# First expert product of an attention and mixture-of-experts kernel: eight quarter products against Strassen's seven

## The chip, the cores and the metric

The kernel runs on one core of a Trainium2 chip. The metric is the device time of one execution in microseconds (us); the time before is the median of three runs. A core has TensorE (PE, matrix products), VectorE (DVE), ScalarE (ACT), GpSimd (POOL) and SyncE (SP, which here only issues DMAs). Each works through its own queue in order and waits on semaphores for the others.

## The reference

A windowed attention (plain windows for half of the heads, dilated ones for the others) feeds a mixture of eight experts, of which each token takes its two best:

```python
    noisy_logits = logits + noise_scale * noise
    top2 = np.argpartition(-noisy_logits, 2, axis=1)[:, :2]
    ...
    for e in range(E):
        for k in range(2):
            mask = top2[:, k] == e
            ...
            h = np.maximum(x[mask] @ w1[e], 0.0)
            out[mask] += top2_w[mask, k, None] * (h @ w2[e])
```

There are 4608 tokens of 512 features; W1 is 512 x 1024 and W2 1024 x 512 per expert. All is float32. The two expert products are made in float32r on TensorE from a high and a low part of each operand: high x high + high x low + low x high, so three matmuls stand for one.

## The kernel before, in words

**Stages.** Attention comes first (slots 0 to 51 of an order written by hand, about 235 us in the profile), with gating and the writing of the token table `tab` threaded through it. Then come eight experts, one after the other, each with a fixed capacity of tokens (`CAPS`: 1216 three times, 1184 twice, 1152 three times), cut into tiles of 128 tokens and into three blocks of 3, 4 and 2 to 3 tiles (`BLS`).

**An expert's work.** For each tile `gather` (L751) fetches rows of x with indirect DMAs from GpSimd: four of 32 rows each for experts 1 to 7 (L766), two for expert 0 (L758), after a small `pace` instruction (L297) that waits for a recent result. `xsplit` (L771) transposes the tile (DVE, L783; TensorE for expert 0, L780), casts it to the high part (ACT, L785) and subtracts for the low part (DVE, L786). `up` (L802) makes the first product of a block: for each of eight slices of 128 hidden features twelve matmuls into one PSUM bank (L814), then a ReLU on ACT (L818) and the low part on DVE (L820). `down` (L868) calls `down_tile` (L841) per tile: 24 matmuls of 512 columns (L856), the scaling into y on DVE (L865), and puts a scatter into `pend`, which adds the rows to `out` by an indirect DMA from GpSimd (L833) and is emitted one tile later. A last tile of at most 64 rows is "stacked": 16 matmuls instead of 24. Weights come through two staging buffers `ws` (L683, L698) and are split into high (ACT, L694, L707) and low (DVE, L696, L709).

**What sets the order.** Each engine executes in the order in which the Python program emits. That order is a planner's: `plan(t, f)` (L884) puts f on a heap, `tick(cols)` (L891) advances a clock `now` by cols/2400 us whenever matmuls are emitted, and emits what has come due. For experts 1 to 7 `plan_x` (L794) plans one gather per 9 us and the split of a tile `LAG` = 15 us later; blocks 0 of x have a buffer of their own, blocks 1 and 2 another each, so a block is split while others are multiplied. The experts are interleaved: up block 0, down block 2 of the expert before, up 1, down 0, up 2, down 1. y has a pool of three buffers (L1048). The index loads of the next expert (L735 to L740) and their copies on GpSimd (L745) are planned in the same way.

**Expert 0.** Its tokens are gathered as the gating goes on: tiles 0 to 2 from the first units of attention, tiles 3 to 6 (up to `SPLITS[2]`) after the third unit, the rest at the end of gating. Its first block needs tiles 0 to 2.

Of the kernel before, what the change touches and what calls it, by code (L numbers as in the profile page):

```python
# [9 lines left out]
F32 = mybir.dt.float32  # L10
F32R = mybir.dt.float32r
# [24 lines left out]
NWARM = 24  # L36
SL_W1 = 5
# [3 lines left out]
US_W2 = 3.0, 3.5  # L41
LAG = 15
US_X = (17, 52)
# [3 lines left out]
def attention_moe_kernel(ctx, tc, qt, kp, kd, vpl, vdl, w_gate, w_noise, noise, w1, w2, out, CAPS=(1216, 1216, 1216, 1184, 1184, 1152, 1152, 1152), SPLITS=(0, 384, 896)):  # L47
# [13 lines left out]
    NBL = [max(bl[i][3] for bl in BLS) for i in range(3)]  # L61
# [192 lines left out]
    def setup_c():  # L254
# [3 lines left out]
        free = [late["stage"].tile([128, FF], I32, name="free", tag="ws") for _ in range(2)]  # L258
# [421 lines left out]
    ST = {}  # L680
    W1, W2 = {}, {}

    def stage_w1(e, kc):  # L683

        s = late["stage"].tile([128, FF], F32, name="ws", tag="ws")
        sync.dma_start(s, w1[0][128 * kc:128 * kc + 128] if type(e) is int else
                       row(w1, e).rearrange("(q c d) f -> c q d f", q=4, c=4)[kc])
# [10 lines left out]
    def stage_w2(e, fc):  # L698
        s = late["stage"].tile([128, 2, DM], F32, name="ws2", tag="ws")
        sync.dma_start(s, row(w2, e)[256 * fc:256 * fc + 256].rearrange("(c p) d -> p c d", p=128))  # L700
        ST[2, fc] = s

    def split_w2(fc):
        s = ST.pop((2, fc))
        a = late["wp2"].tile([128, 2, DM], F32R, name=f"w2h{fc}")
        b = late["wp2"].tile([128, 2, DM], F32R, name=f"w2l{fc}")
        scalar.copy(a, s)  # L707
        W2[fc] = (a, b)
# [513 lines left out]
```

## Time and profile before

| | |
|---|---|
| median of three runs | 1046.4 us (1044.11 to 1051.29) |
| span of the profiled execution | 1109.4 us |
| span of attention, expert 0, experts 1 to 7 | 235.7, 129.5, 734.2 us |
| mean granted TensorE clock | 0.966 |
| HBM read, written | 92.11 MB, 39.54 MB |

The profile is of one execution, whose own time is its span of 1109.4 us, 63 us over the median of the runs; the page gives no other time for it. The views used below: the page (busy time of each engine), the busy time by stretches (for each stretch its length, then busy time and number of instructions of PE, PEld, DVE, ACT and POOL, the granted clock, the DMA share and GB/s; for one source line PE and PEld alone), the groups by form (count, busy us, mean ns, idle time before them and what ended it), and the timeline (start, duration, what, and in brackets the idle time before it with its releaser).

### The profile page before, as it was taken

Reading aid. Unit: us, or ns where it says so; the run is one execution under the profiler, and the core shown is the slowest. Engines: PE = TensorE matmul, PEld = TensorE weight load, DVE = VectorE, ACT = ScalarE, POOL = GpSimd, SP = SyncE. Lnnn points to the kernel's source line nnn. Section 1 sums busy time; section 2 is a strip of 40 time slices with the busy share of each in tenths; the row PEclk is TensorE's granted clock in tenths of the full one; section 3 lists DMA queues with packets and bytes.
Section 4 is the critical chain, followed back from the end, with each engine's and each line's share of the span. In section 5 each row is a group of like instructions: output and inputs, shape, how many; then the busy total and the mean of one; then the engine's idle time right before and its main releaser. Section 6 shows DMA issues by size and latency. Waiting matters only on the chain. (4 is left out here: it accounts for less than half of the span.)

```text
span 1109.4 us, 18401 instructions
## 1 busy us (share of the span) xinstructions
PE 1015.0 (91%) x7278; PEld 853.6 (77%) x7279; DVE 463.9 (42%) x1060; ACT 319.8 (29%) x612; POOL 527.7 (48%) x723
## 2 busy tenths in 40 slices
PE   5896776686999899999999999999999999999996
PEld 3774655465779789878988898788978898888885
DVE  6773535644224444334433433434343344333221
ACT  6673433531113232222222222212231213222110
POOL 6004243356866545664635564455456455553112
PEclk9998887887999999999999999999999999999999
DMA  7798687465243432633353334333433443353123
GB/s 275 254 345 292 193 270 251 122 205 161 44 90 76 102 101 48 139 60 103 65 117 68 97 72 101 82 79 85 97 83 81 104 68 102 62 129 58 32 30 46
DMA packets 77530, 132.91 MB, mean 120 GB/s; under 512 B 29968, under 2 KB 39616, under 8 KB 76160
## 3 DMA queue, kind: packets, MB, share of 16 engines
q1 hardware_dynamic: 55088, 92.55, 26.3%
q0 software_dynamic: 22352, 39.15, 19.6%
q8 instruction: 58, 0.95, 0.4%
q14 instruction: 32, 0.26, 0.1%
HBM read 92.11 MB, written 39.54 MB: 119 GB/s over the span
## 5 line engine op out<-in xcount | busy, mean ns | idle before, releaser
L814 PE MATMUL up<-x,w1h 128*128 128x512 f32 (+4 forms) x1536 | 397.5, 345 | 8.8 <-DVE hl L820 5.8
L766 POOL DMA_INDIRECT g<-xs,ixi x258 | 264.5, 1025 | 84.5 <-issue 79.1
L814 PEld LDWEIGHTS up<-x,w1h 128*128 128x128 f32 x1536 | 272.7, 189 | 36.4 <-DVE hl L820 7.6
L814 PE MATMUL up<-x,w1l 128*128 128x384 f32 (+4 forms) x768 | 264.1, 344 | 1.8 <-DVE w1l L696 1.1
L856 PE MATMUL dn<-w2h,hh 128*128 128x512 f32 x576 | 226.7, 394 | 2.0 <-DVE y L865 1.3
L856 PE MATMUL dn<-w2h,hl 128*128 128x512 f32 x576 | 225.3, 391 | 1.1 <-issue 1.1
L856 PE MATMUL dn<-w2l,hh 128*128 128x512 f32 x576 | 225.5, 391 | 0.6 <-issue 0.6
L820 DVE SCALAR_TENSOR_TENSOR hl<-up,hh 128x384 fp32r<-128x384 f32 (+2 forms) x192 | 106.1, 556 | 228.0 <-ACT hh L818 177.1
L833 POOL DMA_INDIRECT out_rows<-y,ixs x67 | 107.8, 1609 | 189.3 <-DVE y L865 158.3
L818 ACT ACTIVATE hh<-up 128x384 fp32r<-128x384 f32 (+4 forms) x192 | 94.2, 498 | 274.7 <-PE up L814 193.9
L814 PEld LDWEIGHTS up<-x,w1l 128*128 128x128 f32 x768 | 145.7, 190 | 14.7 <-DVE w1l L696 1.8
L856 PEld LDWEIGHTS dn<-w2h,hh 128*128 128x128 f32 x576 | 109.0, 189 | 25.6 <-DVE y L865 2.4
L856 PEld LDWEIGHTS dn<-w2h,hl 128*128 128x128 f32 x576 | 108.8, 189 | 24.0 <-issue 1.1
L856 PEld LDWEIGHTS dn<-w2l,hh 128*128 128x128 f32 x576 | 109.0, 189 | 22.6 <-issue 0.8
L865 DVE TENSOR_SCALAR y<-dn,ixs 128x512 f32<-128x512 f32 x63 | 46.9, 748 | 143.4 <-PE dn L856 114.9
L785 ACT CAST x<-xr 128x512 fp32r<-128x512 f32 x67 | 40.5, 605 | 189.9 <-DVE xr L783 158.5
L619 POOL DMA_INDIRECT tab<-en,si x72 | 72.2, 1002 | 30.7 <-issue 16.4
L696 DVE TENSOR_TENSOR w1l<-ws,w1h 128x1024 fp32r<-128x1024 f32 x32 | 38.8, 1217 | 94.8 <-ACT w1h L694 61.6
L297 POOL COPY spacer<-hh 1x1 f32<-1x1 f32 x72 | 24.2, 336 | 102.0 <-ACT hh L818 101.7
L694 ACT CAST w1h<-ws 128x1024 fp32r<-128x1024 f32 x32 | 33.0, 1048 | 115.9 <-DMA ws<-in_moe_w 115.8
L786 DVE TENSOR_TENSOR x<-xr,x 128x512 fp32r<-128x512 f32 x67 | 44.7, 666 | 18.0 <-ACT x L785 15.9
L783 DVE STREAM_TRANSPOSE xr<-g 128x512 f32<-128x512 f32 x67 | 45.7, 682 | 0.0
(184 smaller groups left out, 856.0 us busy)
## 6 DMA issues: line engine op xcount, KB each, us to landing
ws<-in_moe_w SPq DMA_DIRECT2D x64, 512.0 KB
out_rows<-zero SPq DMA_DIRECT2D x38, 256.0 KB
vd<-in_vdl SPq DMA_DIRECT2D x24, 390.0 KB
vp<-in_vpl SPq DMA_DIRECT2D x16, 585.0 KB
qt<-in_qt SPq DMA_DIRECT2D x14, 576.0 KB
xs<-x SPq DMA_DIRECT2D x24, 256.0 KB
kt<-in_kd SPq DMA_DIRECT2D x16, 320.0 KB
g<-xs,ixi POOLq DMA_INDIRECT x258
```

Source lines behind the costliest of these rows:

```text
L619: ins = gpsimd.indirect_dma_start(out=tab, out_offset=bass.IndirectOffsetOnAxis(ap=si[:, kq, t:t + 1], axis=0), in_=en[:, kq, t], in_offse ...
L696: return lambda: vector.tensor_tensor(b, s, a.bitcast(F32), op=OP.subtract)
L766: gpsimd.indirect_dma_start(out=g[:, j], out_offset=None, in_=xq, in_offset=bass.IndirectOffsetOnAxis(ap=IX[e][1][:, r0 // 32 + j:r0 // 32 ...
L783: vector.transpose(xr[:, :, 0:rn].rearrange("p c (g t) -> p g c t", t=32), g[:, 0:n].rearrange("p g (c d) -> p g c d", d=32))
L785: scalar.copy(xh[:, :, o:o + rn], xr[:, :, 0:rn])
L786: return lambda: vector.tensor_tensor(xl[:, :, o:o + rn], xr[:, :, 0:rn], xh[:, :, o:o + rn].bitcast(F32), op=OP.subtract)
L814: tensor.matmul(p[:, 0:n], lhsT=a[:, 128 * f:128 * f + 128], rhs=b[:, kc, 0:n], start=(i == 0), stop=(i == 11))
L818: scalar.activation(hh[:, f, 0:n], p[:, 0:n], AF.Relu)
L820: vector.scalar_tensor_tensor(hl[:, f, 0:m], p[:, 0:m], 0.0, hh[:, f, 0:m].bitcast(F32), op0=OP.max, op1=OP.subtract)
L833: ins = gpsimd.indirect_dma_start(out=out, out_offset=bass.IndirectOffsetOnAxis(ap=sc[0:rn, t, 1:2], axis=0), in_=y[0:rn], in_offset=None, ...
L856: tensor.matmul(p[0:rn], lhsT=a[:, f, o:o + rn], rhs=b[:, f % 2], start=(i == 0), stop=(i == 23))
L865: vector.tensor_scalar(y[0:rn], p[0:rn], wsc, None, op0=OP.mult)
```

## The change

The product X W1 of a block is made by Strassen's scheme (in the form with fifteen additions) on 2 x 2 quarters: the 512 input features in two halves, the 1024 hidden features in two halves, and each tile's tokens in two halves. Seven quarter products take the place of eight. There are two blocks per expert, of five tiles (`NA`) and of the rest, and expert after expert without interleaving. Sums of quarters are made of W1 (on GpSimd for experts 1 to 7) and of x (on DVE) before the splits; `up` handles the hidden features in four steps j, each with seven products of six matmuls over half of the block's tokens, keeps three partial results per step in SBUF (pool `yt`, four buffers, shared with y), and interleaves the products of two steps. The first tile of `down` is begun inside the end of `up`. x has one buffer for all blocks. W1 is loaded by quarters of its columns. The scaling into y moves from DVE to ACT. Gathers, splits, weights and indices become generators that wait for conditions (a buffer free, an `up` over) and for planner times.

```diff
+US_LOAD = 4.5
+US_GATHER = 4.8
+US_LAG = 9.0
...
-US_W2 = 3.0, 3.5
-LAG = 15
-US_X = (17, 52)
+NA = 5
...
-        cuts = [0, 3, 7, len(tl_)]
-        BLS.append([(cuts[i], cuts[i + 1], 128 * cuts[i], min(cap, 128 * cuts[i + 1]) - 128 * cuts[i]) for i in range(3)])
+        BLS.append([(0, NA, 0, 128 * NA), (NA, len(tl_), 128 * NA, cap - 128 * NA)])
...
+    def stage_w1(e, w, j, kk):
+        s = ST[w, j, kk] = stage()
+        d = s[:, 0:512].rearrange("p (i h f) -> p i h f", i=2, h=2)
...
+        for q in range(4):
+            src = row(w1, e)[128 * q:128 * q + 128].rearrange("(h k d) (i j f) -> d i h k j f", h=2, k=2, i=2, j=4)
+            for i in range(2):
+                sync.dma_start(d[32 * q:32 * q + 32, i], src[:, i, :, kk, j])
+    def sums_w1(w, j, kk, eng):
+        s = ST[w, j, kk]
+        a = s[:, 0:512].rearrange("p (i h f) -> p i h f", i=2, h=2)
+        b = s[:, 512:896].rearrange("p (o f) -> p o f", o=3)
+        eng.tensor_tensor(b[:, 0], a[:, 1, 0], a[:, 1, 1], op=OP.add)
+        eng.tensor_tensor(b[:, 1], b[:, 0], a[:, 0, 0], op=OP.subtract)
+        eng.tensor_tensor(b[:, 2], a[:, 0, 1], b[:, 1], op=OP.subtract)
+        eng.tensor_tensor(a[:, 1, 0], a[:, 0, 0], a[:, 1, 0], op=OP.subtract)
+    def split_w1(w, j, kk):
...
+        t = W1[w, j]
+        scalar.copy(t[:, 0, :, kk], s)
+        def low():
+            vector.tensor_tensor(t[:, 1, :, kk], s, t[:, 0, :, kk].bitcast(F32), op=OP.subtract)
+            ready1[w, j] += 1
+        return low
...
-        scalar.copy(xh[:, :, o:o + rn], xr[:, :, 0:rn])
-        return lambda: vector.tensor_tensor(xl[:, :, o:o + rn], xr[:, :, 0:rn], xh[:, :, o:o + rn].bitcast(F32),
-                                            op=OP.subtract)
+        q = ra.rearrange("p c (h t) -> p c h t", h=2)
+        b = r[:, 512:512 + 6 * m].rearrange("p (o k t) -> p o k t", o=3, k=2)
+        vector.tensor_tensor(b[:, 0], q[:, 0:2, 1], q[:, 0:2, 0], op=OP.subtract)
+        vector.tensor_tensor(b[:, 1], q[:, 2:4, 1], b[:, 0], op=OP.subtract)
+        vector.tensor_tensor(b[:, 2], q[:, 2:4, 0], b[:, 1], op=OP.subtract)
+        vector.tensor_tensor(q[:, 0:2, 1], q[:, 2:4, 1], q[:, 0:2, 1], op=OP.subtract)
+        b = b.rearrange("p o k t -> p (o k) t")
+        xa = [x[:, z, 0:8, o:o + m].rearrange("p (h c) t -> p c h t", h=2) for z in range(2)]
+        xb = [x[:, z, 8:14, o:o + m] for z in range(2)]
+        scalar.copy(xa[0], q)
+        scalar.copy(xb[0], b)
+        def low():
+            vector.tensor_tensor(xa[1], q, xa[0].bitcast(F32), op=OP.subtract)
+            vector.tensor_tensor(xb[1], b, xb[0].bitcast(F32), op=OP.subtract)
+            done[e, bi] = done.get((e, bi), 0) + 1
+        return low
...
-        pool = late["xp0" if bi == 0 else "xp"]
-        t = pool.tile([128, 2, 4, NBL[bi]], F32R, name="x", tag="raw" if bi == 0 else f"x{bi}")
-        X[e, bi] = (t[:, 0], t[:, 1])
...
+        X[e, bi] = late["xp"].tile([128, 2, 14, HN], F32R, name="x", tag="x")
...
-            p = late["mps"].tile([128, 512], F32, name="up", tag="up", bufs=3)
-            i = 0
-            for kc in range(4):
-                wh, wl = W1[kc]
-                for a, b in ((wh, xh), (wh, xl), (wl, xh)):
-                    tensor.matmul(p[:, 0:n], lhsT=a[:, 128 * f:128 * f + 128], rhs=b[:, kc, 0:n],
-                                  start=(i == 0), stop=(i == 11))
-                    i += 1
-            tick(12 * n)
-            scalar.activation(hh[:, f, 0:n], p[:, 0:n], AF.Relu)
...
+    def up(e, bi, n, tail=None):
...
+        def mm(p, j, a, b, start):
+            w = W1[e, j]
+            for kk in range(2):
+                for i, (y, z) in enumerate(((0, 0), (0, 1), (1, 0))):
+                    tensor.matmul(p, lhsT=w[:, y, a, kk], rhs=x[:, z, 2 * b + kk, 0:N], start=start and kk == 0 and i == 0,
+                                  stop=kk == 1 and i == 2, skip_group_check=True)
+            tick(6 * N)
+        def keep(p):
+            t = late["yt"].tile([128, 512], F32, name="yt", tag="yt")[:, 0:N]
+            scalar.copy(t, p)
+            return t
...
+        for j in range(5):
+            i = j - 1
+            if j < 4:
+                while e != "o" and ready1.get((e, j), 0) < 2:
+                    tick(600)
+                P[j] = gps.tile([128, 512], F32, name="upg", tag="tin")[:, 0:N] if more and j % 2 else bank("p", 2)
+                mm(P[j], j, 0, 0, True)
+            if i >= 0:
+                high(i, 1, U2[i])
+            if j < 4:
+                S1[j] = keep(P[j])
+            else:
+                part()
+            if i >= 0:
+                mm(P[i], i, 2, 2, False)
+                low(i, 1, U2.pop(i))
+                add(M5[i], P[i])
+            if j < 4:
+                Q[j] = bank("q", 1)
+                mm(Q[j], j, 4, 4, True)
+            else:
+                part()
+            if i >= 0:
+                high(i + 4, 1, M5[i])
+            if j < 4:
+                M5[j] = keep(Q[j])
+                R[j] = bank("r", 1)
+                mm(R[j], j, 1, 1, True)
+            if i >= 0:
+                low(i + 4, 1, M5.pop(i))
+            if j < 4:
+                add(S1[j], R.pop(j))
+            if i >= 0:
+                mm(P[i], i, 3, 6, False)
+                if bi == 1:
+                    free1[i] = e
+            if j < 4:
+                high(j, 0, S1[j])
+            if i >= 0:
+                high(i + 4, 0, P[i])
+            if j < 4:
+                mm(P[j], j, 5, 5, False)
+                if j == 0 and pend:
+                    pend.pop(0)()
+                low(j, 0, S1.pop(j))
+            else:
+                part()
+            if i >= 0:
+                low(i + 4, 0, P.pop(i))
+            if j < 4:
+                U2[j] = keep(P[j])
+                if e != "o":
+                    mk = gp_.tile([1, 1], F32, name="mk", bufs=4)
+                    scalar.copy(mk, P[j][0:1, 0:1])
+                    late["x"] = mk
+                mm(Q[j], j, 6, 3, False)
+                add(U2[j], Q.pop(j))
+        over.add((e, bi))
...
+        y = late["yt"].tile([128, DM], F32, name="y", tag="yt")
...
-            vector.tensor_scalar(y[0:rn], p[0:rn], wsc, None, op0=OP.mult)
+            scalar.mul(y[0:rn], p[0:rn], wsc)
...
+    late["hp"] = ctx.enter_context(tc.tile_pool(name="hp", bufs=1, reuse_waits="tile"))
+    late["yt"] = ctx.enter_context(tc.tile_pool(name="yt", bufs=4, reuse_waits="tile"))
...
+    def weights(kk):
+        for e in range(E):
+            if e:
+                yield lambda e=e: (e - 1, 1) in begun
+            for j in range(0 if e else 2, 4):
+                stage_w1(EID[e], e, j, kk)
+                yield now[0] + US_LOAD
+                sums_w1(e, j, kk, gpsimd if e else vector)
+                yield now[0] + (2.2 if e else 0.8)
+                if e:
+                    yield lambda e=e, j=j: free1.get(j, -1) >= e - 1
+                low = split_w1(e, j, kk)
+                yield now[0] + 1.2
+                low()
+                yield now[0] + 0.3
+            if e:
+                for f in range(4 * kk, 4 * kk + 4):
+                    stage_w2(EID[e], e, f)
+                    yield now[0] + US_LOAD
+                    yield lambda e=e: (e - 1, 1) in downs
+                    low = split_w2(e, f)
+                    yield now[0] + 0.9
+                    low()
+                    yield now[0] + 0.2
...
+    def gathers():
+        for e in range(1, E):
+            yield lambda e=e: e in index
+            for t in range(len(TLS[e])):
+                yield lambda: held_g[0] < 4
+                gather(e, t)
+                got[e, t] = now[0]
+                held_g[0] += 1
+                yield now[0] + US_GATHER
+    def splits():
+        for e in range(E):
+            for bi in range(0 if e else 1, 2):
+                yield lambda e=e, bi=bi: (e - 1 + bi, 1 - bi) in over
+                new_x(e, bi)
+                yield now[0] + 0.5
+                for t in range(BLS[e][bi][0], BLS[e][bi][1]):
+                    yield lambda e=e, t=t: (e, t) in got
+                    yield max(now[0], got[e, t] + US_LAG)
+                    low = xsplit(e, bi, t)
+                    held_g[0] -= 1
+                    yield now[0] + 1.6
+                    low()
+                    yield now[0] + 2.4
...
+    def indices():
+        for e in range(1, E):
+            yield lambda e=e: (e - 1, 0) in begun
+            yield now[0] + (42 if e == 1 else 24)
+            new_idx(e)
+            idx_dma(e, 0, CAPS[e])
+            yield now[0] + (12 if e == 1 else 9)
+            idx_copy(e, 0, CAPS[e])
+            index.add(e)
...
+        for bi in range(2):
+            t0, t1, _, n = BLS[e][bi]
+            while done.get((e, bi), 0) < t1 - t0:
+                tick(600)
+            begun.add((e, bi))
+            first = down_gen(e, bi, t0)
+            up(e, bi, n, first)
+            down(e, bi, first)
+            if bi:
+                downs.add((e, 1))
```

More of the change, by code (lines that the diff above doesn't have):

```diff
@@ L257, in setup_c @@
         NR = ET // 16
-        free = [late["stage"].tile([128, FF], I32, name="free", tag="ws") for _ in range(2)]
+        free = [late["stage"].tile([128, 896], I32, name="free", tag="ws") for _ in range(2)]
         pr = free[0][:, 0:3 * NR].rearrange("p (a b) -> p a b", a=3)
@@ L698, in stage_w2, with stage @@
[L698 to L708, printed above, removed]
-        return lambda: vector.tensor_tensor(b, s, a.bitcast(F32), op=OP.subtract)
+    def stage():
+        return late["stage"].tile([128, 896], F32, name="ws", tag="ws")
@@ L894, in tick, with go @@
             heappop(due)[2]()
+        for c, g in list(waiting):
+            if c():
+                waiting.remove((c, g))
+                go(g)
+    waiting = []
+    def go(g):
+        try:
+            c = next(g)
+        except StopIteration:
+            return
+        if callable(c):
+            if c():
+                go(g)
+            else:
+                waiting.append((c, g))
+        else:
+            plan(c, lambda: go(g))
     fill = {}
@@ L929, in later, with first_tiles @@
             at(slot[0] + d, f)
[L931 to L932 removed]
+    held_g, got = [0], {}
+    def first_tiles(a, b):
+        for t in range(a, b):
+            while held_g[0] >= 4:
+                yield 1
             yield from wait_turn()
@@ new lines, in first_w2 @@
+    def first_w2(fs):
+        held_g[0] += 1
+        for f in fs:
+            stage_w2(0, 0, f, lambda: gp_.tile([128, 4, 128], F32, name="g").rearrange("p a b -> p (a b)"))
+            yield now[0] + US_LOAD + 0.5
+            low = split_w2(0, f)
+            yield now[0] + 0.9
+            low()
+            yield now[0] + 0.3
+        held_g[0] -= 1
+    def gathers():
[5 more added lines that the diff above has]
+                got[e, t] = now[0]
+                held_g[0] += 1
+                yield now[0] + US_GATHER
@@ new lines, in some_of_slots, with rest @@
+    def some_of_slots():
+        for i in range(min(6, len(backlog))):
+            pace(i == 0)
+            backlog.pop(0)()
+    experts[0] = True
+    for kk in range(2):
+        plan(0.1 + 0.6 * kk, lambda kk=kk: go(weights(kk)))
+    def rest():
+        gens.append(totals())
+        gens.insert(0, first_tiles(NA, len(TLS[0])))
+    gens.append(idx_late(list(gens), SPLITS[2], CAP, rest))
+    for i in range(36):
+        plan(i, some)
+    plan(2.5, some_of_slots)
+    plan(20, lambda: gens.append(rest_of_slots()))
@@ new lines, in attention_moe_kernel @@
+    plan(36, drain)
+    plan(36.1, numbers)
+    while done.get((0, 0), 0) < NA:
+        some()
+        tick(1200)
+    for fs in ((0, 1), (4, 5), (2, 3), (6, 7)):
+        go(first_w2(fs))
+    for g in (gathers(), splits(), indices()):
+        go(g)
+    for e in range(E):
+        for bi in range(2):
[8 more added lines that the diff above has]
+                downs.add((e, 1))
```

293 lines of the change are left out of this document (126 added, 167 removed).

## The prediction

> **What bounds the kernel now.** I read the page first, then the busy time by stretches, then the groups by form, then TensorE's and GpSimd's order of time.
>
> ```profile
> PE 1015.0 (91%) x7278; PEld 853.6 (77%) x7279; DVE 463.9 (42%) x1060; ACT 319.8 (29%) x612; POOL 527.7 (48%) x723
> ```
> ```profile
> 235.70:365.20 129.50, 117.64 (x562) 99.57 (x561) 49.40 (x161) 25.25 (x47) 86.52 (x129) 0.93 0.46 118
> 365.20:1099.40 734.20, 723.74 (x3593) 623.49 (x3592) 284.33 (x452) 172.10 (x289) 365.90 (x454) 1.00 0.38 82
> ```
> After 235.7 us of attention the first expert takes 129.5 us and the other seven 734.2 us; in these TensorE is busy 723.7 us (first pair of numbers), GpSimd 365.9 (last pair). So TensorE sets the time, and GpSimd is half idle on average. The up-projection and one stretch of down, each alone:
>
> ```profile
> 601.30:623.70 22.40, 22.36 (x96) 17.81 (x96) 1.00 0.42 111
> 640.10:652.90 12.80, 12.80 (x96) 12.70 (x95) 1.00 0.24 43
> 989.50:1006.10 16.60, 16.60 (x96) 16.45 (x95) 1.00 0.34 76
> 852.40:863.60 11.20, 11.20 (x96) 11.12 (x95) 1.00 0.27 48
> 532.90:547.00 14.10, 14.10 (x96) 13.96 (x95) 1.00 0.25 48
> ```
> ```profile
> 516.60:532.90 16.30, 16.30 (x72) 13.29 (x71) 1.00 0.37 83
> ```
> Divided by their 96 matmuls: 0.233 us at 512 columns, 0.133 at 288, 0.173 at 384, 0.117 at 256, 0.147 at 320. It goes on falling to 256 columns, so weight loads do not bound it there. Down: 16.3/72 = 0.226, a tile of 24 matmuls 5.43 us. At these rates experts 1 to 7 need 360.4 (up: 53.1, 51.8 or 50.2 by capacity) + 342.1 (63 tiles) + 14.5 (four tails of 16 matmuls) = 717.0 us; the other 17 us are waits.
>
> **The product.** A block now takes 168 matmuls at half its tokens: 320 columns 24.7 us; 288, 272 or 256 columns 22.4, 21.0 (rate between its neighbours) or 19.6. Up falls to 47.1, 45.7 or 44.3 us per expert: 47.9 us less in eight, 41.9 in experts 1 to 7, which then need 675.1.
>
> **Its evacuation.** Per quarter of F: seven ACT and seven DVE passes over 320 columns.
>
> ```profile
> L818 ACT ACTIVATE hh<-up 128x320 fp32r<-128x320 f32 x24 | 10.4, 437 | 45.7 <-PE up L814 29.9 <-issue 15.8
> L820 DVE SCALAR_TENSOR_TENSOR hl<-up,hh 128x384 fp32r<-128x384 f32 x64 | 35.1, 554 | 67.7 <-ACT hh L818 35.0 <-issue 32.7
> ```
> ACT 7 x 0.44 = 3.1, DVE about 7 x 0.5 = 3.4 us, beside 42 matmuls = 6.2 us. Each bank is asked for again two products (1.76 us) after it was left. W2's splits (eight of 0.69 us on DVE) still fit: 19 of 24.7 us. I cost it at nothing; without that cover it is 0.5 us a quarter, 32 us in all.
>
> **The x blocks.** There is one x buffer now, so a block's tiles are split only after `up` is over.
>
> ```profile
> L783 DVE STREAM_TRANSPOSE xr<-g 128x512 f32<-128x512 f32 x63 | 44.2, 702 | 0.0
> L786 DVE TENSOR_TENSOR x<-xr,x 128x512 fp32r<-128x512 f32 x63 | 43.3, 687 | 18.0 <-ACT x L785 15.9 <-issue 2.1
> L785 ACT CAST x<-xr 128x512 fp32r<-128x512 f32 x63 | 39.1, 620 | 185.8 <-DVE xr L783 155.5 <-DVE y L865 25.5 <-DVE hl L820 2.3
> L605 DVE TENSOR_TENSOR oh<-oh,y 128x144 f32<-128x144 f32 x2 | 0.6, 297 | 0.0
> ```
> A tile: transpose 0.70, four sums of 128 columns at 0.28, two casts 1.1, two lows 1.24, in turn across two engines: 4.2 us, 4.6 with hand-overs. Five are 23 us, emitted one per 5.12 us between the tiles of `down`, with ACT's scaling of y ahead of each cast. The last cast stands behind the last y: TensorE waits about 2 us before block 1 (experts 1 to 4), 4 before block 0, 7 before block 0 where block 1 has only four tiles: 43 us, inside the next chain.
>
> **GpSimd's order is where I think it breaks.** A gather is allowed only when a split has freed one of four g buffers, so all gathers fall into the `down` phases, between the scatters; and y now shares four yt buffers with the copies that `up` makes of its products.
>
> ```profile
> 525.10 1.60 POOL L833 DMA_INDIRECT out_rows<-y,ixs  x1 [3.11 <-issue]
> 526.12 0.62 POOL L297 COPY spacer<-hh 1x1 f32<-1x1 f32 x1
> 527.00 1.02 POOL L766 DMA_INDIRECT g<-xs,ixi  x1 [0.26 <-issue]
> 528.32 0.98 POOL L766 DMA_INDIRECT g<-xs,ixi  x1 [0.30 <-issue]
> ...
> 530.86 0.95 POOL L766 DMA_INDIRECT g<-xs,ixi  x1 [0.30 <-issue]
> 531.80 0.09 POOL L832 MEMSET spacer<- 1x1 f32 x1
> 532.11 1.62 POOL L833 DMA_INDIRECT out_rows<-y,ixs  x1 [0.23 <-issue]
> ```
> From scatter to scatter 7.0 us: 1.9 for the scatter, 5.1 for a tile's gather. A tile of `down` lasts 5.43, so GpSimd falls behind there. The last scatter of the kernel, alone, shows when a y buffer is free again (DMA share and GB/s are the last two columns):
>
> ```profile
> 1100.80:1101.80 1.00, 0.00 (x0) 0.00 (x0) 0.00 (x0) 0.00 (x0) 0.98 (x1) 1.00 0.00 0
> ...
> 1102.80:1103.80 1.00, 0.00 (x0) 0.00 (x0) 0.00 (x0) 0.00 (x0) 0.00 (x0) 1.00 1.10 90
> ...
> 1104.80:1105.80 1.00, 0.00 (x0) 0.00 (x0) 0.00 (x0) 0.00 (x0) 0.00 (x0) 0.59 0.16 27
> ```
> Bytes move until 4 to 5 us after its start; I take 5.
>
> With the buffers taken in rotation, the copy of M1 of quarter 1 (S1[1]) gets the slot of the block's last y, and TensorE's product P[1](5,5), ninth of `up`, waits for that copy. I count from the end of `up`; tile 0 of `down` ends at 1.4, tile k 5.43k later, y 0.6 later (its scaling moves from DVE to ACT, priced like ACT's cast of 512 columns).
>
> Before block 1: behind y1 (ready at 7.4) GpSimd has its scatter 1.9, the index copies 1.7, and, by the planner's times, a0 5.1, y2 1.9, a1 5.1, y3 1.9, a2 5.1, a3 5.1 (a0 to a3: the next expert's tiles). y4 starts at 35.2 and has landed at 40.2. TensorE is there at 23.1 + 9 products of 0.80, 0.75 or 0.70 = 30.3, 29.9 or 29.4. Lost: 9.9, 10.3, 10.8, twice each: 62 us.
>
> Before the next block 0: from 2.0 on, four scatters 7.6, five gathers 25.5, and W1's sums of the last quarter. GpSimd's two-input sums are not in the trace; bounds for one are these:
>
> ```profile
> L745 POOL TENSOR_SCALAR ixi<-ixt 32x38 int32<-32x38 int32 x8 | 1.8, 224 | 9.3 <-DMA ixt<-tab 8.9
> L745 POOL TENSOR_SCALAR ixi<-ixt 32x36 int32<-32x36 int32 x12 | 4.4, 367 | 0.6
> L181 POOL CAST mask<-m 128x1152 bf16<-128x1152 f32 x1 | 1.2, 1172 | 2.2 <-DVE ige L171 2.2
> ```
> Between 0.22 and 1.17 us for 128 columns; I take 0.37, nearest in length, so 3.0 for eight. The last y starts at 38.1, lands at 43.1, where TensorE is there at 1.4 + three tiles + a tail of 3.6 = 21.3, and nine products of 0.88 = 29.2: 13.9 us. With four tiles in block 1: 41.2 against 25.6, 15.6 us. Five and two such places: 101 us.
>
> **The clock.** A long stop of TensorE costs twice:
>
> ```profile
> 253.70 0.20 PE L573 MATMUL posp<-ob,tri 128*128 128x24 bf16 x1 [4.93 <-DVE ob L558]
> ...
> 254.94 0.84 PE L814 MATMUL up<-x,w1h 128*128 128x384 f32 x2
> ...
> 255.90 0.84 PE L814 MATMUL up<-x,w1h 128*128 128x384 f32 x2
> ...
> 258.65 0.51 PE L814 MATMUL up<-x,w1h 128*128 128x384 f32 x2
> ...
> 259.18 0.51 PE L814 MATMUL up<-x,w1h 128*128 128x384 f32 x2
> ```
> After 4.9 us idle a turn of three matmuls takes 0.96 us (254.94 to 255.90), later 0.53; from 253.8 to 258.6 five turns go by: 2.1 us lost. Thirteen stops: 27 us. The Trainium skill (TensorE: Matmul & The Clock Gate, Part 1) has the clock halved after about 3.4 us of idleness and for about 3.4 us of work; the trace agrees in kind. By it the x waits over 3.4 us count too, some 20 stops of 1.7, an estimate of 34 us.
>
> **The start.** Block 0 of expert 0 now has five tiles; tiles 3 and 4 are gathered after attention:
>
> ```profile
> 238.32 1.00 POOL L758 DMA_INDIRECT g<-xs,ixf  x1 [6.96 <-DMA ws<-in_moe_w]
> 242.16 0.96 POOL L758 DMA_INDIRECT g<-xs,ixf  x1 [0.30 <-issue]
> ```
> Tile 4's ends at 243.1; with some 2.5 us to land and a 5 us split `up` starts near 250, not 235.7. But expert 0 took 129.5 us against 53.1 + 48.9 + 3.6 = 105.6, much of it gate work that now runs inside this wait. I take 5 us net, between 0 and 15.
>
> **Other moved work.** W1 comes in eight DMA issues per stage on SP, in runs of 512 bytes; bytes are the same and the DMA share is 0.38.
>
> ```profile
> L686 SPq DMA_DIRECT2D ws<-in_moe_w x32: 340/536/672, 153.1 to 971.2; - x32
> ```
> Eight at 0.54 are 4.3 us of SP, with W2's stages and the index loads queued behind; TensorE needs W1 a whole `down` later. I cost it at nothing; uncovered it is 4.3 us a quarter.
>
> **Sum.** Experts 1 to 7: 675.1 + 62 + 101 + 27 = 865.1, 131 more than 734.2. Expert 0: -6.0 + 5 = -1. The profiled execution goes from 1109.4 to 1239. The median of the runs shown, 1046.4, lies 63 below that span; its unprofiled attention and expert 0 must be quicker, which the change leaves alone. 1046.4 + 130 = **1176 us**. Own range: sums at 1.17 us add 45; no sums, no clock loss and landing in 4.2 take off 58: 1118 to 1221.
>
> **Rivals.** (1) One gather of each phase falls behind the last scatter: they are emitted within one tick of each other. 13 x 5.1 = 66 less: 1110. Slower still. (2) GpSimd keeps out of the way, because S1[1] takes another slot; only the x waits are left: 675.1 + 43 - 734.2 - 1 = -17: 1029. It decides if the last y lands before 29 us; for it speaks GpSimd's 48%, against it that its work is bunched. This one is faster. (3) The x splits run ahead as well and only the product changes: -47.9 + 5: 1003. For it speaks that today's waits are 17 us in seven experts; against it the single x buffer. (4) The product is bound by weight loads and gains nothing: against it 0.117 us at 256 columns.
>
> **Chances.** Forecast 0.49, (1) 0.22, (2) 0.13, (3) 0.12; 0.04 near no change, (4) among it. A measurement of this kernel tells about 1% from nothing. Faster by over 1%: 0.25, within 1%: 0.04, slower: 0.71. The range leaves out (3) and what is above 1225: 1025 to 1225; the cases lie on both sides, the likeliest one's own range is the one above.
>
> **What would show it.** Right: ACT's copies into yt waiting for DMA out_rows, TensorE idle some 8 us early in each `up`, GpSimd without gaps in `down`, granted clock below 1 there, 168 matmuls per block at the rates above. Wrong: full clock through experts 1 to 7, and `up` following `down` without a gap.

## The result and the profile after

The changed kernel takes 1294.5 us against 1048.9 for the kernel before (medians of four runs each): a ratio of 1.233 (95% interval 1.227 to 1.239). One of the four runs of the changed kernel took 1956.6 us and is not in the ratio; the other three lie between 1293.8 and 1295.2. The forecast was 1176; the direction was right, the size half of what came.

The profile of the changed kernel, whose span is 1292.2 us: busy time per engine, then the granted clock in 40 slices.

```profile
PE 1012.3 (78%) x7662; PEld 878.6 (68%) x7663; DVE 670.3 (52%) x1765; ACT 519.6 (40%) x1235; POOL 640.5 (50%) x947
...
PEclk9999977898989897989799879988897869896998
```

TensorE was busy for 91% of the span and is for 78%; the clock, full through experts 1 to 7 before, dips in every expert. Busy time by stretches of the changed kernel: attention up to the first `up`, expert 0, experts 1 to 7, the last scatter (columns as before: length, PE, PEld, DVE, ACT, POOL, clock, DMA share, GB/s).

```profile
0.00:213.30 213.30, 163.13 (x3142) 126.35 (x3143) 145.73 (x524) 128.79 (x292) 83.53 (x158) 0.93 0.84 278
213.30:359.80 146.50, 113.39 (x592) 99.99 (x593) 82.73 (x240) 58.73 (x139) 100.24 (x149) 0.90 0.40 98
359.80:1282.80 923.00, 735.74 (x3928) 652.30 (x3928) 441.89 (x1002) 331.37 (x806) 455.15 (x640) 0.89 0.31 64
1282.80:1292.20 9.40, 0.00 (x0) 0.00 (x0) 0.00 (x0) 0.68 (x1) 1.56 (x1) 0.65 0.24 32
```

The same stretches of a later profile of the kernel before (e17), with a span of 1048.9 us:

```profile
0.00:194.70 194.70, 159.90 (x3128) 123.66 (x3129) 129.69 (x446) 122.60 (x276) 75.08 (x140) 0.96 0.88 293
194.70:310.80 116.10, 112.05 (x562) 96.26 (x560) 50.11 (x161) 25.39 (x47) 85.92 (x128) 0.99 0.50 133
310.80:1039.30 728.50, 722.62 (x3593) 623.65 (x3592) 284.77 (x452) 172.49 (x289) 367.17 (x455) 1.00 0.39 83
```

So of the 243 us between the two spans 18.6 are lost before the first `up`, 30.4 in expert 0 and 194.5 in experts 1 to 7. Expert 0's stretch ends where `up` of expert 1 begins, so it holds the wait before that `up`, 14.5 us in the changed kernel. In experts 1 to 7 TensorE stands idle for 187.3 us (923.0 less 735.7) where it stood for 5.9. Executions of one and the same kernel differ ahead of expert 1 (the kernel before began its first `up` at 194.7, 235.7, 238.0 and 242.9 us in four profiles), so the experiments below are compared by experts 1 to 7, which agree within 1.4%: 728.5 to 738.4 before, 923.0 and 926.7 after.

The waits of the changed kernel (engine and tile, what ended them; us in total, times, longest; `upp` and `upg` are products of `up` in PSUM, `yt` ACT's copies of them, `w` the split W1):

```profile
PE upp L856 <- ACT x L823: 119.5, 13, 20.1
ACT yt L862 <- DMA out_rows<-y,ixs: 97.4, 19, 11.0
ACT w L714 <- POOL ws L706: 91.0, 20, 9.3
POOL ws L703 <- DMA ws<-in_moe_w: 77.1, 16, 12.8
PE upg L856 <- ACT yt L862: 64.4, 11, 8.8
```

The second and the last row are the wait that was forecast: ACT's copy of a product waits for y's scatter, TensorE for the copy, 8.8 us at most. The first row is larger: TensorE waits for the block of x, 13 times, up to 20 us. The third and fourth were in no step: ACT's split of W1 waits for GpSimd's sums, and these for W1's data.

How they hang together shows between the last tiles of expert 1 and block 0 of expert 2. ACT's order of time (start, duration, what, idle before it and its releaser):

```profile
474.41 0.69 ACT L993 ACTIVATE y<-dn,ixs 128x512 f32<-128x512 f32 x1 [2.95 <-PE dn L980]
...
483.44 0.94 ACT L714 CAST w<-ws 128x896 fp32r<-128x896 f32 x1 [7.42 <-POOL ws L706]
486.26 0.94 ACT L714 CAST w<-ws 128x896 fp32r<-128x896 f32 x1 [1.88 <-POOL spacer L956]
487.10 0.68 ACT L993 ACTIVATE y<-dn,ixs 128x512 f32<-128x512 f32 x1
490.18 0.62 ACT L823 CAST x<-xr 128x512 fp32r<-128x512 f32 x1 [2.39 <-DVE xr L819]
...
496.14 0.62 ACT L823 CAST x<-xr 128x512 fp32r<-128x512 f32 x1 [3.29 <-DVE xr L819]
```

and GpSimd's:

```profile
474.64 1.62 POOL L957 DMA_INDIRECT out_rows<-y,ixs  x1 [0.22 <-issue]
...
476.56 1.10 POOL L793 DMA_INDIRECT g<-xs,ixi  x1 [0.19 <-DVE x L827]
...
480.47 0.95 POOL L793 DMA_INDIRECT g<-xs,ixi  x1 [0.30 <-issue]
481.45 0.46 POOL L703 TENSOR_TENSOR ws<-ws 128x128 f32<-128x128 f32 x1
...
485.78 0.45 POOL L706 TENSOR_TENSOR ws<-ws 128x128 f32<-128x128 f32 x1
...
486.42 1.62 POOL L957 DMA_INDIRECT out_rows<-y,ixs  x1 [0.16 <-issue]
```

VectorE's:

```profile
484.41 1.09 DVE L717 TENSOR_TENSOR w<-ws,w 128x896 fp32r<-128x896 f32 x1 [7.61 <-ACT w L714]
487.23 1.09 DVE L717 TENSOR_TENSOR w<-ws,w 128x896 fp32r<-128x896 f32 x1 [1.72 <-ACT w L714]
488.24 0.70 DVE L812 STREAM_TRANSPOSE xr<-g 128x512 f32<-128x512 f32 x1
```

GpSimd does scatter, gather, sums, one after the other with gaps of at most 0.3 us. ACT reaches W1's split at 476.0 and waits there until 483.4, because the sums come behind a tile's gather, which nobody needs yet. VectorE waits for ACT at the low part of W1 (7.6 and 1.7 us) and only then transposes the next tile of x (488.2). Behind the split in ACT's order stands a y that would have been due at 479.9 (they come 5.45 us apart), and behind y the casts of the last two tiles of x, which also wait for VectorE: 490.2 and 496.1. TensorE starts at 496.8, 13.3 us after its last matmul of `down`. Each engine waits in order for another that does, in order, something less urgent first.

After such a stop the clock shows this (same columns as the stretches):

```profile
496.00:498.00 2.00, 1.10 (x3) 0.76 (x4) 1.31 (x3) 1.03 (x2) 1.59 (x2) 0.50 1.01 180
498.00:500.00 2.00, 2.00 (x9) 2.00 (x9) 0.00 (x0) 0.43 (x1) 1.39 (x3) 0.50 0.52 114
500.00:502.00 2.00, 2.00 (x14) 2.00 (x13) 0.28 (x1) 0.43 (x1) 1.83 (x3) 0.87 0.25 66
```

Half the clock until about 500.5, 3.7 us after TensorE's start. An `up` that nothing disturbs, the last one of the kernel (256 columns), is as quick as forecast: 18.70/158 = 0.118 us a matmul.

```profile
1240.70:1259.40 18.70, 18.70 (x158) 18.70 (x157) 9.38 (x23) 9.47 (x30) 1.59 (x2) 1.00 0.12 15
```

### The profile page after: what moved, and what is told of

Read it like the earlier page. It is cut to its first block, busy times and chain, and to the rows that moved or that the text cites. A ratio compares the mean times of both kernels' runs of the same rounds, so it can differ in the third digit from the quotient of the medians.

```text
span 1292.2 us, 23119 instructions
## 1 busy us (share of the span) xinstructions
PE 1012.3 (78%) x7662; PEld 878.6 (68%) x7663; DVE 670.3 (52%) x1765; ACT 519.6 (40%) x1235; POOL 640.5 (50%) x947
## 3 DMA queue, kind: packets, MB, share of 16 engines
q0 software_dynamic: 22352, 39.15, 17.2%
## 5 line engine op out<-in xcount | busy, mean ns | idle before, releaser
L980 PE MATMUL dn<-w2h,h 128*128 128x512 f32 x1152 | 371.6, 396 | 9.2 <-ACT y L993 6.6
L856 PE MATMUL upp<-x,w 128*128 128x320 f32 (+3 forms) x864 | 163.3, 329 | 138.4 <-ACT x L823 119.5
L980 PEld LDWEIGHTS dn<-w2h,h 128*128 128x128 f32 x1152 | 220.2, 191 | 56.6 <-ACT y L993 7.5
L856 PEld LDWEIGHTS upp<-x,w 128*128 128x128 f32 x864 | 140.8, 211 | 151.2 <-ACT x L823 124.8
L980 PE MATMUL dn<-w2l,h 128*128 128x512 f32 x576 | 227.6, 395 | 0.0
L856 PE MATMUL upg<-x,w 128*128 128x320 f32 (+3 forms) x672 | 120.7, 319 | 72.3 <-ACT yt L862 64.4
L856 PEld LDWEIGHTS upg<-x,w 128*128 128x128 f32 x672 | 106.6, 205 | 79.2 <-ACT yt L862 67.0
L856 PE MATMUL upq<-x,w 128*128 128x320 f32 (+3 forms) x768 | 141.1, 324 | 2.7 <-DVE yt L866 2.4
L717 DVE TENSOR_TENSOR w<-ws,w 128x896 fp32r<-128x896 f32 x64 | 69.7, 1100 | 118.3 <-ACT w L714 107.6
L856 PEld LDWEIGHTS upq<-x,w 128*128 128x128 f32 x768 | 126.9, 213 | 3.4 <-DVE yt L866 2.7
L980 PEld LDWEIGHTS dn<-w2l,h 128*128 128x128 f32 x576 | 110.2, 191 | 21.3
L619 POOL DMA_INDIRECT tab<-en,si x72 | 71.6, 994 | 31.6 <-issue 14.7
L703 POOL TENSOR_TENSOR ws<-ws 128x128 f32<-128x128 f32 x56 | 30.5, 544 | 114.5 <-DMA ws<-in_moe_w 77.1
```

The costliest lines, as they stand in the source:

```text
L619: ins = gpsimd.indirect_dma_start(out=tab, out_offset=bass.IndirectOffsetOnAxis(ap=si[:, kq, t:t + 1], axis=0), in_=en[:, kq, t], in_offse ...
L717: vector.tensor_tensor(t[:, 1, :, kk], s, t[:, 0, :, kk].bitcast(F32), op=OP.subtract)
L856: tensor.matmul(p, lhsT=w[:, y, a, kk], rhs=x[:, z, 2 * b + kk, 0:N], start=start and kk == 0 and i == 0, stop=kk == 1 and i == 2, skip_gr ...
L980: tensor.matmul(p[0:rn], lhsT=h[:, a, f, r0:r0 + rn], rhs=b, start=(i == 0), stop=(i == 23), skip_group_check=True)
```

## The experiments

The theory after the result: GpSimd's queue in `down` (gathers, W1's sums, scatters in turn) sets both kinds of wait (G). Rivals: W1's eight DMA issues and late data (D, later W for all of W1's way), and the chain of x's splits itself, there being one x buffer (X). Whole times of e2 to e18 are single runs in us, each with one run of the kernel before on the same chip behind the comma; "1 to 7" is the time of experts 1 to 7 in the trace, "block 0" the span of the waits just ahead of block 0 of experts 2 to 7.

| run | whole, before beside it | 1 to 7 | block 0 |
|---|---|---|---|
| after; e5 again | 1294.5; 1298.3, 1045.2 | 923.0; 926.7 | 12.9 to 20.1; 12.9 to 21.7 |
| e2 sums on VectorE | 1355.9, 1122.1 | 920.7 | 16.8 to 20.0 |
| e3 gathers in `up` | 1270.6, 1122.1 | 848.7 | 11.0 to 13.2 |
| e4 both | 1302.4, 1122.1 | 875.5 | 15.0 to 17.2 |
| e6 four issues | 1294.4, 1045.2 | 920.8 | 14.6 to 20.1 |
| e7 four issues, gathers in `up` | 1180.3, 1045.2 | 814.6 | 8.6 to 13.2 |
| e8 gathers in `up`, W1 planned late | 1262.2, 1045.2 | 899.8 | 4.8 to 10.5 |
| e10 as e7, W1 planned late | 1297.3, 1120.0 | 870.7 | 5.3 to 8.8 |
| e11 as e7, splits in a pipeline | 1208.6, 1120.0 | 798.5 | 4.2 to 6.4 |
| e12 as e11, W1 planned late | 1274.4, 1120.0 | 863.0 | 0.9 to 4.5 |
| e13 W1 left out | 1196.5, 1049.6 | 846.8 | 5.6 to 8.9 |
| e14 a quarter of the gathers | 1146.3, 1049.6 | 791.5 | 7.0 to 14.7 |
| e15 both left out | 1096.7, 1049.6 | 747.3 | 5.6 to 8.8 |
| e16 as e11, W1 left out | 1059.7, 1049.6 | 714.3 | 0 to 2.4 |
| e18 as e11, sums on VectorE | 1182.1, 1051.0 | 820.7 | 2.9 to 14.4 |

**The kernel before again: e1, e9, e17.** No edit.

> The kernel before, unchanged, for a second profile. The profiled execution that the prediction was reckoned against lasted 1109.4 us, its runs 1046. Theory as predicted: the missing 63 us lie in attention and expert 0 alone, so the first up starts near 213 us (where the changed kernel's starts), expert 0 takes about 90 us, and experts 1 to 7 again 734. Rival: part of the 63 lies in experts 1 to 7, so that the base of the sum for the product was too long.

> The kernel before once more, for a profile of an execution near its median of 1046 us; both profiles so far were of executions of 1109 and 1127 us, in which the first up began at 235.7 and 242.9 us and experts 1 to 7 took 734 and 738. If the 63 us lie before expert 1, the first up begins near 200 here, expert 0 takes 100 to 110 and experts 1 to 7 again 734 to 738.

> The kernel before, for the stretch up to expert 1: three profiles so far, all on executions of 1109 to 1127 us, had the first up at 236 to 243 us and expert 1 at 365 to 379. If this one is near 1046: experts 1 to 7 again 734 to 738, expert 1 at about 299 (1046 less 735, 10 of scatter and 2 around the span), the first up near 198, 15 us before that of the changed kernel, since tiles 3 and 4 of its first block are gathered only after attention.

The first two were again long executions (1129.1 and 1117.3 us; first `up` at 242.9 and 238.0, experts 1 to 7 in 738.4 and 735.3). e17 took 1050.6: first `up` at 194.7, expert 0 in 116.1, experts 1 to 7 in 728.5. Against the profile on which the forecast was reckoned that is 41.0, 13.4 and 5.7 us less: the missing 63 us do lie ahead of expert 1, nearly all. On the three chips of these runs two executions each were close (1129.1 and 1122.1, 1117.3 and 1120.0, 1050.6 and 1051.0 us), so the long and the short ones went with the chip.

**The changed kernel again: e5.** No edit.

> The changed kernel as it is, on the chip of the next three, since chips were seen to differ before expert 1 (the first up began at 213 us in one place, at 243 to 263 in others). Expected: experts 1 to 7 again 923 us within 1%, whatever attention does; if they differ by more, comparisons across chips do not hold.

926.7 us against 923.0: comparisons by experts 1 to 7 hold.

**W1's sums on VectorE: e2.**

```diff
-                sums_w1(e, j, kk, gpsimd if e else vector)
+                sums_w1(e, j, kk, vector)
```

> Changed kernel with W1's sums on VectorE instead of GpSimd. Theory G (GpSimd's queue in `down` sets both waits; ACT's split of W1 stands behind GpSimd's sums, and y and the casts of x behind that): 17 us of GpSimd less per expert; ACT's waits L714 <- POOL (120 us in 24 places) go; TensorE's wait before block 0 falls from 13-20 us to 6-10; the wait before block 1 (8.7 us, ACT yt <- DMA out_rows) stays. About 60 us less: 1235. Theory X (the one x buffer: five splits of 4.6 us in turn set the wait): no gain before block 0, 1290.

A miss: 920.7, and the wait before block 0 longer. The waits of this kernel:

```profile
PE upp L856 <- ACT x L823: 115.0, 8, 20.0
DVE ws L703 <- DMA ws<-in_moe_w: 102.2, 31, 5.7
ACT yt L862 <- DMA out_rows<-y,ixs: 74.6, 14, 11.0
```

ACT no longer waits for GpSimd, but VectorE now waits 102 us for W1's data, with x's transposes and sums behind it in its own order. So the price is not GpSimd's time for the sums; it is that an engine waits at them for their data, with urgent work behind.

**Gathers only while `up` runs: e3.**

```diff
-                yield lambda: held_g[0] < 4
+                yield lambda e=e, t=t: held_g[0] < 4 and (inup[0] or (e, int(t >= NA)) in X)
...
+            inup[0] = True
             up(e, bi, n, first)
+            inup[0] = False
```

> Changed kernel with the gathers held back until `up` runs (GpSimd stands idle there for 27 us), but for tiles of the block that is being split; sums stay on GpSimd. Theory G: ACT yt <- DMA out_rows (97 us in 19 places) goes to under 15, the 8.7 us before block 1 with it, and the sums of the last quarters run earlier, so the wait before block 0 falls to 6-10 us: 100 to 130 us less, 1165 to 1195. Theory X: only the yt waits go, 60 to 70 us with the clock: 1225 to 1235.

```profile
PE upp L856 <- ACT x L823: 88.3, 12, 13.2
ACT w L714 <- POOL ws L706: 58.7, 22, 10.1
ACT yt L862 <- DMA out_rows<-y,ixs: 2.1, 3, 1.7
```

The wait for y's scatter is gone, 97.4 to 2.1 us, without touching the buffers that y and the copies share: the gathers made the scatter late. The wait for x fell by 31 us only; 848.7 lies between what G and X gave.

**Both: e4.** The two diffs together.

> Both edits: gathers in `up`, W1's sums on VectorE. Theory G: what is left per boundary is the end of the split chain, 2 to 4 us before each block, and the granted clock rises to 0.96 and more: experts 1 to 7 about 735 us, whole 1080 to 1100. Theory X: the splits still last 23 us against a `down` of 27 with y in between: wait before block 0 still 10 us and more, 1180 and above.

875.5, worse than e3 alone: as in e2, sums on VectorE hold up x. G in its first form, with the sums as GpSimd's burden, has fallen.

**Four DMA issues per stage of W1: e6, and with gathers in `up`: e7.**

```diff
-        for q in range(4):
-            src = row(w1, e)[128 * q:128 * q + 128].rearrange("(h k d) (i j f) -> d i h k j f", h=2, k=2, i=2, j=4)
-            for i in range(2):
-                sync.dma_start(d[32 * q:32 * q + 32, i], src[:, i, :, kk, j])
+        src = row(w1, e).rearrange("(q h k d) (i j f) -> i h k j q d f", q=4, h=2, k=2, i=2, j=4)
+        for i in range(2):
+            for h in range(2):
+                sync.dma_start(d[:, i, h], src[i, h, kk, j])
```

> Changed kernel with a quarter stage of W1 loaded by four DMA issues instead of eight (the same bytes and the same runs of 512 bytes, one issue for all four groups of 32 partitions). Theory D (the eight issues, 0.51 us each, make a pair of stages land 9 to 10 us after the planner's start where it reckons 4.5, so that the sums and the split of W1 stand in GpSimd's, ACT's and VectorE's order before their data and hold up x and y): a pair lands 4 us sooner, TensorE's wait before block 0 falls from 13 to 20 us to 8 to 13, experts 1 to 7 from 923 to about 870. Theory G (GpSimd's scatters and gathers alone): waits as they were, 910 to 925.

> Four issues and the gathers held to `up`. With held gathers alone experts 1 to 7 took 848.7 us and the waits before block 0 were 10 to 13 us. Theory D: these fall to about 5, experts 1 to 7 to 790 to 800. Theory X (the one x buffer; splits in turn): 840 to 850.

Alone it gives nothing (920.8; GpSimd still waits 76.0 us for W1's data, where it waited 77.1): sums that stand behind gathers don't profit from earlier data. With the gathers out of the way it gives 34 us (848.7 to 814.6), less than D expected and more than X.

**W1 planned later: e8, e10, e12.** The planner's landing time of W1's stages raised from 4.5 to 10 us (e8) or 7 us (e10, e12) in experts 1 to 7; where W2's split then is not out in time, `down_tile` waits for it in the planner.

```diff
-                yield now[0] + US_LOAD
+                yield now[0] + (10.0 if e else US_LOAD)
...
+            while e != "o" and (e, f) not in W2:
+                tick(600)
```

> Gathers held to `up`, eight issues, and only the planner's figure for the landing of a W1 stage raised from 4.5 to 10 us in experts 1 to 7, so that its sums and split are put behind the x and y work that is ready earlier. If the standing in the engines' order is what costs (D): the wait before block 0 falls from 10 to 13 us to 4 to 6, experts 1 to 7 from 848.7 to 790 to 800, though SP is as busy as before. If the loads themselves are too slow: the wait moves to TensorE's wait for W1's quarters in `up`, gain under 15 us.

> Four issues, gathers in `up`, and the planner's landing of W1's stages raised from 4.5 to 7 us (experts 1 to 7). With four issues and held gathers these experts took 814.6 us. Theory D (ACT stands at W1's split before data, x and y behind it): ACT's waits L714 <- POOL fall from 84 us to under 40, the wait before block 0 from 9 to about 6, 785 to 795 us. Theory X (the split chain itself, 4.6 us a tile with W1's 8.5 us in between, is longer than `down`): 805 to 815.

> All of it: four issues, gathers in `up`, later planning of W1, splits in a pipeline. If the causes add: wait before block 0 about 2 us, experts 1 to 7 740 to 755. If either theory has the whole wait: as the better of the two runs before this one.

All three lost about 50 to 65 us against the same kernel without it. The wait before block 0 did fall (to 0.9 to 4.5 us in e12), but W2 is loaded behind W1 through the same two buffers and now comes late, as two rows of e8 show, of a kind that only these three kernels have:

```profile
PE dn L982 <- ACT w2h L731: 33.3, 19, 3.0
PE dn L982 <- DVE w2l L734: 20.2, 26, 2.2
```

The two rows are 54 us, as much as e8 lost (51). In e10 and e12 they are 30 and 39 of 56 and 65 us lost; the rest was not traced. Later planning moved the wait here, it didn't hide it.

**The splits of x in a pipeline: e11.**

```diff
+                last = None
...
-                    yield now[0] + 1.6
-                    low()
-                    yield now[0] + 2.4
+                    if last:
+                        last()
+                    last = low
+                    yield now[0] + 3.4
+                last()
```

> Four issues, gathers in `up`, and the splits of x in a pipeline: VectorE's transpose and sums of the next tile are put ahead of the two low parts of the last one, so that VectorE does not wait for ACT's casts (3.2 us a tile where the chain in turn is 4.6). Theory X: five tiles end 6 us sooner, the wait before block 0 falls from 9 to about 3, experts 1 to 7 from 814.6 to 755 to 770. Theory D: at most 2 us per boundary, 795 to 805.

798.5: the wait before block 0 fell from 9 to 13 us to 4 to 6, most of what X expected, but about half of the gain was lost again, to longer waits inside `up`, and the time is the one that D gave. Of the variants that compute everything this is the quickest in experts 1 to 7, and still slower than the kernel before.

**W1 left out, gathers left out: e13 to e16.** e13 and e16 leave out loads, sums and split of W1 in experts 1 to 7, which use expert 0's W1; e14 fetches 32 of a tile's 128 rows and transposes these four times; e15 does both. So all four leave out work that the result needs and tell of the time alone.

```diff
-            for j in range(0 if e else 2, 4):
+            for j in range(4) if e else ():
+                W1[e, j] = W1[0, j]
+                ready1[e, j] = 2
+            for j in () if e else range(2, 4):
...
-        for j in range(rn // 32):
+        for j in range(1):
...
-                             g[:, 0:n].rearrange("p g (c d) -> p g c d", d=32))
+                             g[:, 0:1].to_broadcast([128, n, 128]).rearrange("p g (c d) -> p g c d", d=32))
```

> Changed kernel that leaves out W1 of experts 1 to 7: no loads, no sums, no split; their products use expert 0's W1. Base: experts 1 to 7 in 923 to 927 us, TensorE's wait before block 0 of 13 to 21 us, 8.7 to 10.7 us early in `up` of block 1. Theory W (what W1's stages put into the queues holds up x): the wait before block 0 falls to 4 to 6, the one of block 1 stays, experts 1 to 7 about 840. Theory G (gathers and scatters on GpSimd): both waits keep most of their length, 890 to 910. Theory X (the chain of splits): before block 0 about 9 is left, 860 to 880.

> Changed kernel that gathers only 32 of a tile's 128 rows in experts 1 to 7 (one indirect transfer per tile where there are four; the transpose reads these rows four times): GpSimd 1.3 us per tile where it takes 5.1. Theory G: the wait of block 1 goes (6 x 8.7 us and 2 us of clock each), the wait before block 0 falls by the two or three gathers in it to 4 to 8 us, experts 1 to 7 to 790 to 810. Theory W: block 1 as with G, before block 0 still 10 and more, 835 to 855.

> Both left out: W1 of experts 1 to 7 as with no reload, and a quarter of the gathers. What is left is the chain of splits alone. Theory X: 23 us of splits in turn against a `down` of 27 to 29 that starts them at once: 2 to 4 us before each block, 4 to 7 before block 0 of the short ones, 730 to 745. If more than 760, a cause is still missing.

> The best version so far (gathers in `up`, splits in a pipeline; experts 1 to 7 in 798.5 us) without W1 of experts 1 to 7, which shows what W1's way through the engines still costs in it. Theory W: waits before block 0 under 2 us and in `up` under 1: 710 to 725. If x or y set the rest: 770 and above.

Experts 1 to 7 of e13, e14, e15 and e16, one row of each (columns as above):

```profile
338.40:1185.20 846.80, 722.52 (x3928) 646.28 (x3928) 389.98 (x954) 288.26 (x758) 360.20 (x448) 0.92 0.29 55
```
```profile
343.80:1135.30 791.50, 710.06 (x3928) 630.88 (x3928) 445.89 (x1002) 328.94 (x805) 291.56 (x466) 0.95 0.31 60
```
```profile
338.50:1085.80 747.30, 698.12 (x3928) 625.67 (x3928) 389.19 (x954) 287.46 (x757) 180.59 (x274) 0.96 0.27 47
```
```profile
334.00:1048.30 714.30, 692.30 (x3929) 621.47 (x3927) 389.33 (x958) 288.31 (x759) 375.98 (x458) 0.99 0.35 67
```

From the 924.9 mean of after and e5: W1 out 78 us less, three quarters of the gathers out 133, both 178, so they overlap by 34. The times are those of W in e13 and e16 and of G in e14, within 7 us, and e15 took 2 us more than X gave, with longer waits before block 0. The waits of e13 and e15 say which of the two makes which wait:

```profile
ACT yt L862 <- DMA out_rows<-y,ixs: 100.7, 19, 11.0
PE upg L856 <- ACT yt L862: 70.7, 12, 9.1
PE upp L856 <- ACT x L823: 55.5, 13, 8.9
```
```profile
PE upp L856 <- ACT x L823: 54.9, 13, 8.8
...
ACT yt L862 <- DMA out_rows<-y,ixs: 4.4, 3, 1.6
```

Without W1 the wait for y's scatter stays (100.7 us) and the wait for x falls from 119.5 to 55.5; taking the gathers away as well leaves x at 54.9 and ends the other. So the scatter's wait is the gathers', the upper half of x's wait goes with W1, and the lower half is the chain of splits, which no relief of GpSimd shortens. The upper half needs both W1 and the gathers, since cutting the gathers alone (e14) brings the wait for x to 79.9; e16, which also puts the splits in a pipeline, has block 0 wait 0 to 2.4 us. All three theories hold a part. Even e16, with W1 for nothing, is not faster as a whole than the kernel before (1059.7 against 1049.6): its experts 1 to 7 take 714.3 us where that kernel's take 728.5, but its first `up` begins at 216.9, not 194.7.

**What W1 still costs in e11: e18.** e11 with the diff of e2.

> Four issues, gathers in `up`, splits in a pipeline (experts 1 to 7 in 798.5 us), and W1's sums on VectorE instead of GpSimd. If GpSimd's 17 us of sums per expert are what holds up ACT's split of W1 (80 us of waits there): 760 to 775. If it is the loads that come late, VectorE now stands before W1's data in place of GpSimd (as with eight issues, 98 to 102 us of waits) with x's sums behind it: 800 to 830.

```profile
DVE ws L703 <- DMA ws<-in_moe_w: 82.6, 34, 4.4
PE upp L856 <- ACT x L823: 49.0, 8, 14.4
ACT w L714 <- DVE ws L706: 33.6, 19, 3.6
```

820.7, 22 us more than e11: again it is W1's data that come late, and the engine that waits for them passes the wait on. The issues of W1's loads themselves wait for the staging buffer, which VectorE's low part of W1 (L717) frees:

```profile
SPq L697 <- DVE w L717: 331.9, 21, 33.6
```

So part of the lateness may come from the late splits themselves; this is not shown. A third staging buffer would test it, and a second x buffer theory X; neither was tried.

## Why the prediction was wrong

The step that failed is **other moved work**: W1's eight issues and its quarters were put at nothing, since TensorE needs W1 a whole `down` later. TensorE does. But W1's sums and split stand in the orders of GpSimd, ACT and VectorE at the time when the planner thinks that the data have landed, and what stands behind them is needed at once. e13 prices W1's way at 78 us in experts 1 to 7 and, by expert 0's 125.9 us there against 146.5, at 20.6 us up to the start of expert 1. With the gathers cut it is 44 (791.5 to 747.3), in e11 84 (798.5 to 714.3). With W1 truly at nothing (e13) experts 1 to 7 take 118 us more than in e17 (846.8 against 728.5); the forecast without its seven times 3.0 us for W1's sums has 110. So without W1's way the sum nearly comes out for these experts, partly by luck: block 0 is 12 us under its term there, TensorE's busy time 20 over the clock's. The price that the step gave if uncovered, 4.3 us of SP a quarter, was not the mechanism in the changed kernel, where halving the issues changed nothing; it is worth 34 us once the gathers are out of the way (e7).

**The product** was right: 0.118 us at 256 columns against 0.117, and no wait on **evacuation** in e15, where `up` has no stop in twelve of these experts' fourteen blocks. At 320, 288 and 272 columns the median distance between the starts of two matmuls, outside the stretches of half clock, is 0.147, 0.133 and 0.125 us, as reckoned. So the 41.9 us are saved; the waits cost more.

**x blocks** were about right as a chain by itself: 2, 4 and 7 us were forecast (which add to 42, not 43), and e15 measured 1.0 to 1.1, 5.6 and 8.8.

**GpSimd before block 1** was right in mechanism and size: 62 us forecast; in the changed kernel 54.7 us of stops in `up` of block 1 (8.6 to 10.7 in each of six) and 4.2 ahead of it, 58.9. e3 and e14 end this wait by moving or cutting the gathers, as the step has it.

**GpSimd before block 0**: 101 us forecast for seven places. Measured are 96.3 ahead of block 0 of experts 2 to 7 and 13.5 in `up` of these blocks, 109.8, and the 14.5 ahead of expert 1: 124.3. But it did not come by the step's way. The copies were to wait for the last y; instead x comes so late that little is left of that. Without W1 (e13) the seven places take 68.0, where the step without W1's sums has 80.

**The sums' size** was low: 0.37 us each was taken, between bounds of 0.22 and 1.17. The groups of the changed kernel (mean ns behind the comma) have 470 to 676, the same sums on VectorE about 290:

```profile
L703 POOL TENSOR_TENSOR ws<-ws 128x128 f32<-128x128 f32 x56 | 30.5, 544 | 114.5 <-DMA ws<-in_moe_w 77.1 <-DVE h L881 12.7 <-DVE yt L866 10.2
L705 POOL TENSOR_TENSOR ws<-ws 128x128 f32<-128x128 f32 x56 | 37.9, 676 | 4.4
L704 DVE TENSOR_TENSOR ws<-ws 128x128 f32<-128x128 f32 x8 | 2.4, 301 | 0.3
```

**The clock** was mis-sized: 27 us for 13 stops of 2.1. In experts 1 to 7 the trace has 23 stretches of half clock; TensorE is busy in them for 97 us, so 48 are lost, 2.1 a stretch. The size of one was right, and so were thirteen: 13 stretches go with stops of 7.5 us and more (30 us lost). The other ten (18 us) follow stops of 1.9 to 3.3 us, which the step did not count. By the rule of the Trainium skill (TensorE: Matmul & The Clock Gate, Part 1), under which the clock halves after about 3.4 us of idleness, some 20 stops were to count, an estimate of 34 us. The trace agrees in the length of the shortest half-clock stretches, 3.4 us, but not in the idleness before them. Busy time is 60.6 us over the 675.1 of the sum; the other 12 are not the clock, and the kernel before has 5.6 over its 717.0.

**Waits after `up`** were in no step: 16.9 us, part of them before the last products, which are made inside the first tile of `down`, part (6.6 us) for a PSUM bank that ACT, held at W1's split, has not read.

**The start** was missed too. The first `up` comes 18.6 us later and expert 0 is 30.4 longer, 49.0 together; forecast -1. On one chip the first `up` was at 215.0 in a variant of the changed kernel (e18) and at 194.7 before (e17), so the shift of some 14 us that the step began with was about right. What failed is its cover: the slack of expert 0 was 24 us in the profile at hand and is 10.5 in e17 (116.1 against 105.6); most of it belonged to the long execution. And 20.6 of expert 0's 30.4 go when W1 is left out (e13).

**The base** was right as to place: the 63 us lie ahead of expert 1. Sum: 243.3 measured between the spans of e17 and after, 130 forecast. Of the 113 missing, 50 are start and expert 0 (with the 14.5 us before expert 1, which the sum has in experts 1 to 7), 6 experts 1 to 7 before (728.5, not 734.2), and 58 experts 1 to 7 after: clock 21, other busy time over the rates 12, waits after `up` 17, block 0 9, block 1 -3, small gaps the rest.

The range ended at 1225 because its ends were made from the sums' price and the rivals; none of them had W1's way, and neither W1 nor the start, whose own upper end was 15 us, widened it.

## What to carry to other kernels

Cost a moved load not by when its last user needs it, but by what stands behind its first user in each engine's order at the planner's time for it; that user waits for its data and holds up urgent work on every engine that it passes. Where one in-order queue carries urgent and early work (here scatters and gathers), hold the early work back to the stage in which the queue is idle: that alone gave 74 us here. Before a sum is made, see whether the profiled execution is like the runs that will be compared, and give every term put at nothing an upper end in the range.

## What the runs showed of the hardware

A stop of TensorE need not be long to be paid twice. In the first `up` of expert 1 a stop of 2.8 us, which ends at 373.9, is followed by 3.4 us at half clock. After a stop of 1.1 us, which ends at 420.0, the clock stays full (columns as in the stretches above):

```profile
374.20:377.60 3.40, 3.40 (x15) 3.40 (x15) 2.01 (x5) 2.55 (x8) 0.00 (x0) 0.51 0.00 0
420.00:424.00 4.00, 3.94 (x28) 3.73 (x29) 1.12 (x4) 1.45 (x5) 3.14 (x4) 1.00 0.60 86
```

In experts 1 to 7 of the changed kernel every stop of 1.9 us and more has such a stretch, and none of 1.8 us or less has one of its own.

The stretch ahead of expert 0 took 194.7 to 242.9 us for one kernel, with a DMA share of 0.88 in the shortest and 0.71 to 0.73 in the others, while experts 1 to 7 with a share of 0.38 to 0.39 stayed within 1.4%. Where two executions on one chip are on record, they agree within 0.7%; what makes the chips differ was not tried.
